# Four of 128 stores on 14 DMA engines, in shares of nine partitions

## The chip, the cores and the metric

One core of one Trainium2 chip. The metric is the device time of one execution, in microseconds (us), median of the timed runs. The kernel of before was run again beside every kernel, on the same chip.

## The reference, cut to what matters

Attention with one query per head, and its gradients. There are 2 x 32 = 64 heads, 8192 keys each, head size 128, all bf16.

```python
def _fwd_reference(q, k, v):
    scale = q.shape[-1] ** -0.5
    scores = jnp.einsum("bhqd,bhkd->bhqk", q, k) * scale
    p = _softmax(scores, axis=-1)
    return jnp.einsum("bhqk,bhkd->bhqd", p, v)
# returned: the output, and the gradients of q, k and v for a given grad_out
```

K and V are 64 x 2 MB each and are read once. dK and dV have the same size and are written once. That is 268 MB in and 268 MB out, with little arithmetic per byte.

## The kernel before

Per head, K and V are loaded whole into SBUF (128 partitions x 16 KB) from the SyncE queue. Twelve such tiles rotate. When scores, softmax and the reductions are done, VectorE overwrites the K tile with dK and the V tile with dV, in place, and GpSimd issues the store. The next load into that tile waits until the store has landed.

```python
CH = 16                      # rows of one partition per chunk; a tile has NT = 64
NTILE = 12                   # K and V tiles in rotation
load_eng = nc.sync
store_eng = nc.gpsimd

def load(i, w, pieces=(NCH,)):           # w: 0 is K, 1 is V
    h = heads[i]
    t = kvp.tile([P, NT, D], BF16, tag=f"kv{slot_of(i, w)}", name="kvt")
    ...
        pin(load_eng.dma_start(out=t[:, n0:n1, :], in_=src[:, n0:n1, :]))

def outer(i, w, c, ends):
    ...                                  # VectorE writes chunk c of dK or dV into the tile
    if c + 1 in ends:
        at = ends.index(c + 1)
        b0, b1 = (ends[at - 1] if at else 0) * CH, (c + 1) * CH
        dst = (dv_v if w else dk_v)[i]
        pin(store_eng.dma_start(out=dst[:, b0:b1, :], in_=h.tile[w][:, b0:b1, :]))

whole = [NCH]                            # one 2 MB store per tile
last = list(range(1, NCH + 1))           # the last head's are cut in four
...                                      # (all else is cut: transposes, scores, softmax, dQ)
```

## Time and profile before

| | before |
|---|---|
| time, first three runs | 1306.17 us median (1304.99 to 1306.63) |
| span of the profiled run | 1303.1 us |
| busiest compute engine | PE, 89% |
| DMA | 414 GB/s over the span |

The page of the kernel before has busy time by engine in part 1. Part 2 cuts the span into 40 equal slices: the DMA digits are the busy share of the 16 DMA engines in tenths (9 is 90% or more), and the row below is what they moved.

```profile
span 1303.1 us, 42566 instructions
PE 1154.0 (89%) x19268; PEld 873.0 (67%) x19268; DVE 937.5 (72%) x2122; ACT 974.8 (75%) x641; POOL 72.4 (6%) x142
DMA  9999999999999999999999999999999999999965
GB/s 390 423 427 427 427 427 427 428 426 430 427 427 427 427 427 429 427 428 427 429 427 427 429 427 424 418 420 425 421 416 420 419 421 421 418 421 422 394 281 206
```

The DMA engines bound the kernel. The last three slices tell more: 394, 281 and 206 GB/s means that some engines have nothing left to do while another still works.

The waits of the SyncE queue in before (who waits, for whom, us in all, times, longest) show that loads wait for stores:

```profile
SPq L89 <- DMA out_dram<-kvt: 1140.6, 116, 24.2
```

The chain of work that ended last, near its end, in before (start, us, what): the last head's compute hangs on the landing of the last load of V.

```profile
1215.54 49.35 DMA kvt<-in_v_dram
1264.94 1.49 PE tp L166 x16
```

The page has no view by DMA engine, but the trace keeps the sixteen completion steps of each copy, one per engine. Read from there, for 2 MB stores counted from 0 (us from the start of the span):

```
store   first step   15th step   16th step   16th - 15th
  8        125.9       128.9       130.4        1.5
 24        281.5       287.5       293.0        5.6
 64        672.2       684.8       698.5       13.7
112       1155.0      1161.6      1185.1       23.4
```

One engine, the laggard, falls behind by 0.21 us per store (23.4 - 1.5 over 104 stores), while the other fifteen lie within some 15 us. Every load waits for that engine. It gets through a head in 20.25 us; over its 32 packets of 16 KB per head that makes 633 ns each, where the median packet takes 611. At the end of the last load of V, when only it still has load packets, its last 13 took 618 to 655 ns.

### The profile page before, as it was taken

Reading aid. Unit: us, or ns where it says so; the run is one execution under the profiler, and the core shown is the slowest. Engines: PE = TensorE matmul, PEld = TensorE weight load, DVE = VectorE, ACT = ScalarE, POOL = GpSimd, SP = SyncE. Lnnn points to the kernel's source line nnn. Section 1 sums busy time; section 2 is a strip of 40 time slices with the busy share of each in tenths; the row PEclk is TensorE's granted clock in tenths of the full one; section 3 lists DMA queues with packets and bytes.
Section 4 is the critical chain, followed back from the end, with each engine's and each line's share of the span. In section 5 each row is a group of like instructions: output and inputs, shape, how many; then the busy total and the mean of one; then the engine's idle time right before and its main releaser. Section 6 shows DMA issues by size and latency. Waiting matters only on the chain.

```text
span 1303.1 us, 42566 instructions
## 1 busy us (share of the span) xinstructions
PE 1154.0 (89%) x19268; PEld 873.0 (67%) x19268; DVE 937.5 (72%) x2122; ACT 974.8 (75%) x641; POOL 72.4 (6%) x142
## 2 busy tenths in 40 slices
PE   6999998889898888988989888989898898888984
PEld 5777776667676666666766666667676676666662
DVE  2888887677776777767777677676776767777776
ACT  6888887777787777777778777777777777777771
POOL 0000000000000000000000000000000000000001
PEclk9999999899898999989989999898898989999986
DMA  9999999999999999999999999999999999999965
GB/s 390 423 427 427 427 427 427 428 426 430 427 427 427 427 427 429 427 428 427 429 427 427 429 427 424 418 420 425 421 416 420 419 421 421 418 421 422 394 281 206
DMA packets 38517, 539.67 MB, mean 414 GB/s; under 512 B 4544, under 2 KB 4544, under 8 KB 5824
## 3 DMA queue, kind: packets, MB, share of 16 engines
q1 hardware_dynamic: 19040, 268.51, 48.9%
q0 software_dynamic: 19296, 268.44, 48.7%
q8 instruction: 150, 2.46, 0.7%
q14 instruction: 31, 0.25, 0.0%
HBM read 268.47 MB, written 268.47 MB: 412 GB/s over the span
## 4 chain that ended last, share of the span: by engine, by line
issue 80%; DMA 11%; POOL 4%; DVE 2%; PE 1%; POOLq 0%; SPq 0%; DVEq 0%
DMA kvt<-in_v_dram 8%; POOL out_dram L390 4%; DMA out_dram<-kvt 3%; DVE kvt L376 1%; PE tp L166 1%; POOLq L390 0%; PE acc L321 0%; DVE sel L344 0%; PE dpw L177 0%; SPq L89 0%; SPq L96 0%; DVE sel L338 0%; PE sw L177 0%; PE acc L358 0%; DVE pair L252 0%
## 5 line engine op out<-in xcount | busy, mean ns | idle before, releaser
L168 ACT COPY ev<-tp 128x2048 bf16<-128x2048 bf16 x512 | 954.0, 1865 | 300.3 <-PE tp L166 290.6
L166 PE MATMUL tp<-ident_bf,kvt 128*128 128x128 bf16 x8192 | 573.4, 226 | 108.9 <-DMA kvt<-in_v_dram 91.1
L376 DVE TENSOR_TENSOR kvt<-qb,pair 128x2048 bf16<-128x2048 bf16 x512 | 621.1, 1214 | 0.2
L166 PEld LDWEIGHTS <-kvt 128*128 128x128 bf16 x8192 | 501.4, 102 | 116.2 <-DMA kvt<-in_v_dram 95.8
L177 PEld LDWEIGHTS <-ev 128*128 128x128 bf16 x8192 | 242.8, 96 | 211.2 <-issue 164.4
L321 PE MATMUL acc<-kvt,dS_pad 128*64 128x512 bf16 x1024 | 177.2, 430 | 1.3 <-DVE dqT L361 1.3
L321 PE MATMUL acc<-kvt,E_pad 128*64 128x512 bf16 x1024 | 159.8, 392 | 0.0
L177 PE MATMUL dpw<-qdT,ev 128*128 128x1 bf16 x4096 | 140.9, 164 | 12.0 <-DVE qb L159 10.7
L189 DVE TENSOR_REDUCE mp<-sw 128x1 f32<-128x64 f32 x64 | 14.3, 224 | 186.5 <-PE sw L177 186.5
L344 DVE SCALAR_TENSOR_TENSOR sel<-acc,diag,sel 128x128 f32<-128x128 f32 x384 | 134.6, 351 | 13.6
L177 PE MATMUL sw<-qdT,ev 128*128 128x1 bf16 x4096 | 142.5, 164 | 1.1 <-ACT ev L168 1.1
L390 POOL DMA_DIRECT2D out_dram<-kvt x134 | 71.3, 532 | 1219.2 <-DVE kvt L376 1186.8
L321 PEld LDWEIGHTS <-dS_pad 128*64 128x64 bf16 x1024 | 38.5, 113 | 26.9 <-issue 9.4
L229 DVE CAST E_pad<-E_f 128x64 bf16<-128x64 f32 x64 | 12.5, 195 | 60.6 <-ACT E_f L220 60.6
L321 PEld LDWEIGHTS <-E_pad 128*64 128x64 bf16 x1024 | 36.3, 108 | 21.0 <-issue 0.2
L358 PE MATMUL acc<-ones,sel 128*128 128x1 f32 x256 | 43.3, 239 | 6.2 <-DVE sel L344 6.2
L264 PE MATMUL dpw<-ld,ones 128*128 128x1 f32 x256 | 46.3, 250 | 0.1
L338 DVE TENSOR_SCALAR sel<-acc,diag 128x128 f32<-128x128 f32 x128 | 44.0, 344 | 0.0
L358 PEld LDWEIGHTS acc<-ones,sel 128*128 128x128 f32 x256 | 39.0, 193 | 7.3 <-DVE sel L344 7.3
L235 DVE CUSTOM_DVE_ANT_0 junk<-E_f,dpw 128x64 bf16<-128x64 f32 x64 | 14.1, 220 | 40.2 <-PE dpw L177 40.2
L159 DVE CAST qb<-dpw 128x128 bf16<-128x128 f32 x128 | 35.4, 277 | 6.0 <-PE dpw L150 6.0
L264 PEld LDWEIGHTS dpw<-ld,ones 128*128 128x128 f32 x256 | 38.2, 188 | 0.5 <-DVE ld L235 0.5
(42 smaller groups left out, 303.2 us busy)
## 6 DMA issues: line engine op xcount, KB each, us to landing
out_dram<-kvt POOLq DMA_DIRECT2D x126, 2048.0 KB, 40.4
kvt<-in_v_dram SPq DMA_DIRECT2D x64, 2048.0 KB, 49.3
kvt<-in_k_dram SPq DMA_DIRECT2D x63, 2048.0 KB, 49.4
out_dram<-kvt POOLq DMA_DIRECT2D x8, 512.0 KB, 11.3
kvt<-in_k_dram SPq DMA_DIRECT2D x2, 512.0 KB, 4.5
kvt<-in_k_dram SPq DMA_DIRECT2D x1, 1024.0 KB, 7.1
out_dram<-nat SPq DMA_DIRECT2D x2, 16.0 KB, 5.0
qd_nat<-in_q_dram SPq DMA_DIRECT2D x1, 16.0 KB, 6.8
```

The costliest lines, as they stand in the source:

```text
L159: pin(nc.vector.tensor_copy(out=h.qb[w][:], in_=h.qbp))
L166: pin(nc.tensor.transpose(tp[:, t, :], src[:, c * CH + t, :], ident_bf[:]))
L168: pin(nc.scalar.copy(out=ev[:], in_=tp[:]))
L177: nc.tensor.matmul(dst[:, c * CH + t : c * CH + t + 1], lhsT=ev[:, t, :], rhs=qdT[:, w, i : i + 1], start=True, stop=True,)
L189: pin(nc.vector.reduce_max(out=h.mp[:], in_=h.s, axis=AX.X))
L264: nc.tensor.matmul(out, lhsT=ones[:].to_broadcast([P, P]), rhs=col, start=True, stop=True)
L321: nc.tensor.matmul(h.acc[w][g : g + CW, :], lhsT=wts[:, n0 : n0 + CW], rhs=rows[:, n0 : n0 + QT, :].rearrange("p n d -> p (n d)"), start=( ...
L338: nc.vector.tensor_scalar(out=h.sel[:], in0=block, scalar1=diag[:, 0:1], scalar2=None, op0=ALU.mult)
L344: nc.vector.scalar_tensor_tensor(out=h.sel[:], in0=block, scalar=diag[:, b : b + 1], in1=h.sel[:], op0=ALU.mult, op1=ALU.add,)
L358: nc.tensor.matmul(h.acc[w][:, 0:1], lhsT=h.sel[:], rhs=ones[:], start=True, stop=True)
L376: nc.vector.tensor_tensor(out=h.tile[w][:, n0 : n0 + CH, :].rearrange("p n (e t) -> p n e t", t=2), in0=h.qb[w][:] .rearrange("p (e t) -> ...
L390: pin(store_eng.dma_start(out=dst[:, b0:b1, :], in_=h.tile[w][:, b0:b1, :]))
```

## The change

Its intent is to take work off that slow engine. For four heads' dK stores (heads 9, 23, 37, 51), four pieces of two partitions move GpSimd's round-robin cursor over the DMA engines from 0 to 8. Then the other 126 partitions go out as one copy. 126 = 14 x 9, so by the rule that the prediction cites it runs on 14 engines from the cursor on: 8 to 15 and 0 to 5. Engines 6 and 7 are left with one 4 KB piece each in place of 128 KB. `max_dma_last_dim`, in bytes, is given half a row, so rows are cut in two.

```diff
-            pin(store_eng.dma_start(out=dst[:, b0:b1, :], in_=h.tile[w][:, b0:b1, :]))
+            if w == 0 and i % 14 == 9 and ends is whole:
+                spread(dst, h.tile[w])
+            else:
+                pin(store_eng.dma_start(out=dst[:, b0:b1, :], in_=h.tile[w][:, b0:b1, :]))
+
+    def spread(dst, t):
+
+        def put(parts, r0, r1):
+            pin(
+                store_eng.dma_start(
+                    out=dst[parts, r0:r1, :],
+                    in_=t[parts, r0:r1, :],
+                    max_dma_last_dim=(r1 - r0) * D,
+                )
+            )
+
+        pin(store_eng.inc_swdge_sem([], [], mode="reset_dge_cursor"))
+        for m in range(4):
+            put(slice(P - 2, P), m * NT // 4, (m + 1) * NT // 4)
+        put(slice(0, P - 2), 0, NT)
```

## The prediction

> **What bounds it now.** The DMA engines, and among them one. The page's DMA row stands at 9 tenths in 38 of 40 slices, at 414 GB/s over the span; the busiest compute engine, PE, is at 89%. In the SP queue's waits, loads wait 1140.6 of 1303 us for stores to land, so each load starts when the slowest share of an earlier store is in.
>
> The trace keeps sixteen completion steps of every DMA. In store 8 the sixteenth comes 1.5 us after the fifteenth; in store 24, 5.6; in store 64, 13.7; in store 112, 23.4. So one engine falls behind 0.22 us per store all through; the other fifteen lie within some 10 us. Heads come 20.25 us apart by the laggard. A 16 KB packet takes 611 ns at the median; the laggard's 32 packets a head give 20.25/32 = 633 ns. The last load of V has its fifteenth step at 1243.0 us and its sixteenth at 1264.9; in the chain of waits the final head's compute (38 us) hangs on that landing. The last store: fifteenth step 1295.1, sixteenth 1301.1. In the last three slices bandwidth falls to 394, 281 and 206 GB/s: fifteen engines run dry.
>
> **What the change does.** For four heads' dK (9, 23, 37, 51) engines 6 and 7 carry 4 KB each in place of 128 KB. The Trainium skill (DMA: Bandwidth & Descriptors, section "Why a DMA increments its semaphore by 16 and not by 1") says that GpSimd copies not spread over all 16 run on k consecutive engines from a cursor, k the largest divisor up to 16. Four two-partition pieces move the cursor from 0 to 8; then 126 partitions on 14 engines take 8 to 15 and 0 to 5. The cap on the last dim halves the rows (an 8 KB packet costs 309 ns here, so no loss) and presumably keeps the copy off the all-sixteen path. No trace here shows the cursor yet.
>
> Which engine lags cannot be read here. The same page ("Latency and other measured facts") calls 7 and 15 usually slower; the change is sensible only if the laggard is 7 or 6.
>
> - Removed from the laggard: 4 x 124 KB = 31 packets x 633 ns = 19.6 us.
> - Added to the others: 16 or 20 KB per store, 4 to 5 packets x 611 ns = 2.4 to 3.1 us in all.
> - Added on GpSimd: four issues of 0.53 us and a cursor reset per such store; it idles 7 to 12 us between stores. Off the path.
>
> **On the critical path.** The laggard would land the last load at about 1245.3, the others at 1243.0 + 3 = 1246: balanced, about 19 us gained. The tail gives 2 to 4 us more, since the final stores no longer queue behind a backlog; the small dQ and O stores then end it (now 1298.7 against 1301.1). Together about 21.5 us.
>
> **Prediction: 1284.5 us**, 80% range 1280 to 1302. Faster by over 2%: 0.07; within 2%: 0.91; slower: 0.02.
>
> **What would show it.** After each of the four stores the gap from fifteenth to sixteenth step drops by about 5 us, ending near 0 to 3; heads come every 19.9 us on average; the last three slices keep higher bandwidth.
>
> **What would make it wrong.** The laggard is another engine, or cursor or split differ (one in five): then the lag stays or grows, and the time is 1303 to 1312. Nine-partition shares might crowd SBUF ports and make packets slower. The second-slowest engines may lag more once pushed.

## More of the kernel before

The DMA view of before lists issues by line: what moves, the issuing queue, how many, KB each, and the median time from issue to landing.

```profile
out_dram<-kvt POOLq DMA_DIRECT2D x126, 2048.0 KB, 40.4
kvt<-in_v_dram SPq DMA_DIRECT2D x64, 2048.0 KB, 49.3
kvt<-in_k_dram SPq DMA_DIRECT2D x63, 2048.0 KB, 49.4
```

A 2 MB copy at full rate needs about 5 us (2.1 MB / 427 GB/s). Here each takes 40 to 49 us, so several copies stand in the queues of every engine at once.

The waits of GpSimd in before show that it waits for VectorE's results only, never for a landing:

```profile
POOL out_dram L390 <- DVE kvt L376: 1186.8, 127, 32.2
```

## The result, and the profile after

| | before | after |
|---|---|---|
| time | 1305.58 us median (1304.88 to 1306.63, 4 runs) | 1315.10 us median (1314.79 to 1315.35, 4 runs) |
| span of the profiled run | 1303.1 us | 1312.9 us |
| ratio | | 1.0072, 95% interval 1.0055 to 1.0090 |

A ratio is the mean time of one kernel's runs over that of the other's runs of the same rounds, so it is not quite the ratio of the medians. Executions over 1.5% slower than the fastest of the same kernel are left out of the means. The change made the kernel 0.7% slower: 9.5 us lost where 21.5 were to be gained.

The page after, the same lines as of before:

```profile
span 1312.9 us, 42614 instructions
PE 1143.8 (87%) x19268; PEld 867.7 (66%) x19268; DVE 936.5 (71%) x2122; ACT 975.4 (74%) x641; POOL 83.0 (6%) x158
DMA  9999999999999999999999989999999989999993
GB/s 389 426 428 427 426 427 427 427 426 428 428 428 428 428 428 410 425 425 427 429 428 428 427 355 386 418 427 427 429 428 428 428 331 387 423 427 427 428 405 120
```

There are dips at slices 16, 24 and 25, and 33 and 34 (410; 355, 386; 331, 387), and the tail is still there (120). The DMA view after:

```profile
out_dram<-kvt POOLq DMA_DIRECT2D x122, 2048.0 KB, 62.1
kvt<-in_v_dram SPq DMA_DIRECT2D x64, 2048.0 KB, 19.0
kvt<-in_k_dram SPq DMA_DIRECT2D x63, 2048.0 KB, 19.3
out_dram<-kvt POOLq DMA_DIRECT2D x4, 2016.0 KB, 48.7
out_dram<-kvt POOLq DMA_DIRECT2D x16, 8.0 KB, 54.5
```

Stores now stand 62 us in the queues and loads only 19. The waits of the SyncE queue and of GpSimd after:

```profile
SPq L89 <- DMA out_dram<-kvt: 1165.6, 124, 24.4
```

```profile
POOL out_dram L393 <- DVE kvt L376: 903.6, 101, 32.6
POOL out_dram L393 <- DMA out_dram<-kvt: 80.5, 11, 11.0
POOL out_dram L393 <- issue: 50.9, 7, 11.3
POOL out_dram L399 <- DMA out_dram<-kvt: 41.2, 5, 9.6
```

By these lines GpSimd now waits 121.7 us (80.5 + 41.2) for stores to land; the page of before has no such wait. Around the second changed head its timeline after shows it (start, us busy, idle before and what ended it):

```profile
477.09 0.55 POOL L399 DMA_DIRECT2D out_dram<-kvt  x1 [3.59 <-DMA out_dram<-kvt]
487.19 0.55 POOL L399 DMA_DIRECT2D out_dram<-kvt  x1 [9.56 <-DMA out_dram<-kvt]
497.04 0.77 POOL L399 DMA_DIRECT2D out_dram<-kvt  x1 [9.30 <-DMA out_dram<-kvt]
507.45 0.58 POOL L393 DMA_DIRECT2D out_dram<-kvt  x1 [9.64 <-DMA out_dram<-kvt]
```

The trace says why: the stores use eight semaphores in turn, and GpSimd may not reuse one before the store that had it has landed. Five copies in a row take five of the eight while four to seven stores are still in flight. Where the profile prints "DVE" or "issue" after such a wait, the instruction before each of these issues is GpSimd's own wait on a store semaphore. So the printed sum is too low. Counted from the trace instead, as the idle time before every issue that comes within 0.7 us of the landing of the store eight issues earlier, it is 33 issues and 204.3 us (before: one, 1.9 us). This count is used below.

Which engine lags? The completion steps (16th minus 15th, us, by store of the head order; the pieces of a cut store counted as one) and, with them, those of the first experiment:

```
store              18    24    46    52    74    80   102   108   120
before            3.5   5.6   9.9  11.5  15.3  17.5  21.1  21.9  22.9
after             3.4   5.4   9.7  19.9  24.5  26.4  34.3  32.0  20.3
e1 (below)        3.5   1.3   4.0   0.1   4.4   3.1   1.2   3.0   2.2
```

The changed stores are numbers 19, 47, 75 and 103. After the second the lag jumps from 9.7 to 19.9 us, after the third it grows by 1.9, after the fourth it is 2.3 less, and after none does it drop by the 5 us that were expected: the laggard was not relieved. The packet records say more. Each small piece carries data on two engines, and on the fourteen others a packet of 8 B stands in its place. At the last changed head, the latest of these packets, 30 us behind all others and so the laggard's, come at:

```
8 B at 1105.8    8 B at 1107.1    4096 B at 1108.3    8 B at 1109.7      (us, after)
```

So the laggard carried data in the third of the four pieces. The third pair from cursor 0 is 4 and 5. At heads 23 and 37 the order is the same (527.3, 528.6, data at 529.8, 531.2; and 818.2, 819.5, data at 820.7, 821.5). The change left out the pair next to it.

### The profile page after: what moved, and what is told of

Read it like the earlier page. It is cut to its first block, busy times and chain, and to the rows that moved or that the text cites. A ratio compares the mean times of both kernels' runs of the same rounds, so it can differ in the third digit from the quotient of the medians.

```text
span 1312.9 us, 42614 instructions
## 1 busy us (share of the span) xinstructions
PE 1143.8 (87%) x19268; PEld 867.7 (66%) x19268; DVE 936.5 (71%) x2122; ACT 975.4 (74%) x641; POOL 83.0 (6%) x158
## 4 chain that ended last, share of the span: by engine, by line
DMA 36%; another core or an unknown queue 35%; issue 17%; PE 7%; DVE 2%; SPq 1%; POOL 1%; POOLq 0%
DMA kvt<-in_v_dram 17%; DMA out_dram<-kvt 14%; DMA kvt<-in_k_dram 5%; PE tp L166 3%; PE acc L321 2%; DVE kvt L376 1%; SPq L89 1%; PE dpw L177 1%; POOL out_dram L393 1%; PE sw L177 1%; DVE sel L344 0%; POOL out_dram L399 0%; DVE sel L338 0%; PE dpw L264 0%
## 5 line engine op out<-in xcount | busy, mean ns | idle before, releaser
L321 PE MATMUL acc<-kvt,dS_pad 128*64 128x512 bf16 x1024 | 172.8, 421 | 1.8 <-DVE dqT L361 1.8
```

The costliest lines, as they stand in the source:

```text
L321: nc.tensor.matmul(h.acc[w][g : g + CW, :], lhsT=wts[:, n0 : n0 + CW], rhs=rows[:, n0 : n0 + QT, :].rearrange("p n d -> p (n d)"), start=( ...
```

## The experiments

Engines are named by the cursor's count: 0 is where it starts after a reset. No run shows that this count is the chip's own numbering.

### e1: the other pair

```diff
-        for m in range(4):
+        for m in range(3):
             put(slice(P - 2, P), m * NT // 4, (m + 1) * NT // 4)
         put(slice(0, P - 2), 0, NT)
+        put(slice(P - 2, P), 3 * NT // 4, NT)
```

> Same five copies per chosen head as the change, same bytes, but the big copy is issued fourth and one small piece last, so the pair left out is 4 and 5. Theory A (wrong pair: in the trace of the change the lagging engine carried data in the third small piece, so it is 4 or 5 by the cursor's count): the gap from fifteenth to sixteenth step drops by about 5 us at each of the four heads instead of growing by 10, and the laggard saves 19 us; with GpSimd's waits still there I expect 1290 to 1300 us. Rival (the pair does not matter, the loss is all GpSimd's blocked issue or the nine-partition shares): 1313 to 1317 us.

Measured: 1289.19 us median (1288.02 to 1290.40), ratio 0.9882 (0.9868 to 0.9897). Theory A holds, and the time is just under its range. The lag stays at 0.1 to 4.4 us (row e1 of the table above). The same five copies, the same bytes, as long waits of GpSimd for landings (34 issues, 209.6 us, against 33 and 204.3), and only another pair of engines: the sign turns. Its GB/s row:

```profile
GB/s 389 423 427 427 426 427 428 427 427 427 427 427 427 428 428 426 421 427 427 427 427 428 427 427 397 411 427 428 428 427 429 428 412 403 422 427 427 427 427 230
```

In the last three slices it moves 427, 427 and 230 GB/s, where before moved 394, 281 and 206: the sixteen engines now finish nearly together. The wrong pair is shown.

### e2, e3: two copies in place of five

The first changed head sets the cursor, with five copies (e2) or four (e3). Later heads need two: the small copy of 2 partitions runs on the pair, the big one takes the next 14 engines, and 2 + 14 = 16 brings the cursor back.

```diff
-        pin(store_eng.inc_swdge_sem([], [], mode="reset_dge_cursor"))
-        for m in range(4):
-            put(slice(P - 2, P), m * NT // 4, (m + 1) * NT // 4)
+        if first:                        # i == 9
+            pin(store_eng.inc_swdge_sem([], [], mode="reset_dge_cursor"))
+            for m in range(3):           # e3: range(2)
+                put(slice(P - 2, P), 16 * m, 16 * m + 16)
+            put(slice(P - 2, P), 48, NT) # e3: 32
+        else:
+            put(slice(P - 2, P), 0, NT)
         put(slice(0, P - 2), 0, NT)
```

> Pair 6 and 7 as in the change, but with two copies per head (one small, one big) after the first such head, where five set the cursor. Theory B (five copies in a row take five of the eight store semaphores, so GpSimd stands until old stores have landed, stores and then loads start late and all engines run dry): the dips to 331 to 410 GB/s vanish, GpSimd's waits on landed stores shrink from 120 us to under 50, and the time is 1307 to 1310 us, the remainder being 4 extra shares of 16 KB on the lagging engine (2.5 us). Rival (the shares of nine partitions or the 8 KB packets cost the time): stays at 1313 to 1317 us.

> Both: pair 4 and 5 left out and two copies per head (four at the first). If A and B hold, the laggard saves 28 packets x 633 ns = 18 us, no dips, and the tail gives 2 to 4 us: 1284 to 1289 us. If only A holds: about as e1. If only B holds: 1306 to 1309 us.

Measured: e2 1313.62 us (1311.52 to 1317.26), ratio 1.0072 (1.0055 to 1.0090); e3 1290.58 us (1288.28 to 1292.67), ratio 0.9887 (0.9871 to 0.9904). e2 lands in the range of its rival, not of theory B. The deepest dips are gone (lowest slice before the tail 396 GB/s), and its page prints few waits on landings:

```profile
POOL out_dram L393 <- DMA out_dram<-kvt: 24.2, 4, 11.0
POOL out_dram L399 <- DMA out_dram<-kvt: 5.2, 2, 2.7
```

But by the count above 19 issues still waited 137.7 us, so e2 took away only a third of the waits and is a weak test. e3 waited 75.4 us where e1 waited 209.6, and is as fast as e1, not faster. Fewer waits gained nothing here; e4, next, tests the waits directly.

### e4, e5, e11: the side costs alone

No engine is left out, all shares are even and at their usual partitions. e4 cuts the store of the four heads in five copies, e5 cuts its rows in half, e11 does both.

```diff
+        # e4 (e11: the same, with max_dma_last_dim=(r1 - r0) * D)
+        for r0, r1 in ((0, 2), (2, 4), (4, 6), (6, 8), (8, NT)):
+            pin(store_eng.dma_start(out=dst[:, r0:r1, :], in_=t[:, r0:r1, :]))
+        # e5
+        pin(store_eng.dma_start(out=dst, in_=t[:], max_dma_last_dim=NT * D))
```

> For the same four heads the store is cut into five plain 128-partition copies (four of 2 rows, one of 56), all 16 engines, no cursor, no padding. Theory B alone: the dips and GpSimd's waits are there without any uneven share: 1309 to 1315 us. Rival (the loss of the change comes from the uneven shares): 1305 to 1307 us.

> For the change's four heads the store stays one even copy over 128 partitions and 16 engines, but with rows cut into 8 KB packets. Theory (an engine takes turns packet by packet, so half-size store packets give loads twice the bytes for a while; this only shifts stores back and loads forward, no work is added): 1304 to 1307 us, loads landing sooner after issue and stores later. Rival (half-size packets by themselves slow the lagging engine, and explain part of the 9 us): 1308 to 1312 us.

> Five even copies over 128 partitions for the change's four heads, all with rows cut in half: the two side costs of the change together, no engine left out. If they add (e4 2.2 us, e5 1.8 us): 1308 to 1310 us, which with 3.2 us for 80 KB more on the lagging engine accounts for 7 to 8 of the 9.4 us that the change lost. If they do not add: 1306 to 1307 us.

Measured: e4 1306.86 us, ratio 1.0018 (1.0003 to 1.0033); e5 1306.35 us, 1.0014 (0.9999 to 1.0029); e11 1307.31 us, 1.0017 (1.0000 to 1.0033). So the two costs come to about 2 us, alone or together. e4 has GpSimd's waits (32 issues, 211.9 us, as many as after) and the dips in full:

```profile
POOL out_dram L398 <- DMA out_dram<-kvt: 68.9, 9, 9.9
POOL out_dram L393 <- DMA out_dram<-kvt: 27.2, 5, 9.6
GB/s 389 422 427 429 426 426 428 426 429 427 428 428 428 428 427 427 427 428 427 428 428 426 428 383 401 423 427 427 427 427 428 428 333 397 426 427 427 427 422 122
```

383 and 333 GB/s, much as after, yet the kernel loses 2 us. So GpSimd's waits are not what the change lost. Counting the sixteenth steps of loads and stores together, by bytes, the laggard of e4 stays within about 2 us of before all through. So the dips are mostly the other fifteen engines, using up early the slack that they otherwise idle away at the end.

e5 in the DMA view:

```profile
out_dram<-kvt POOLq DMA_DIRECT2D x126, 2048.0 KB, 57.4
kvt<-in_v_dram SPq DMA_DIRECT2D x64, 2048.0 KB, 31.6
```

Stores 40.4 to 57.4 us, loads 49.3 to 31.6, from four stores with half-size packets. The Trainium skill (DMA: Bandwidth & Descriptors, section "Queues, rings and completion order") says that a DMA engine takes turns between its queues packet by packet. This agrees: while store packets are half as big, loads get the larger part of the bytes. What one queue gains the other loses, and the total hardly moves.

### e6, e7: one engine alone

Six heads; 120 partitions run on 15 engines, eight each; engine 4 (e6) or 5 (e7) is left out of that copy. The 8 other partitions move the cursor.

```diff
-        for m in range(4):
-            put(slice(P - 2, P), m * NT // 4, (m + 1) * NT // 4)
-        put(slice(0, P - 2), 0, NT)
+        put(slice(P - 5, P), 0, NT)          # e7: P - 6
+        put(slice(0, P - 8), 0, NT)
+        put(slice(P - 8, P - 5), 0, NT)      # e7: P - 6
```

> Six heads; 15 engines carry 8 partitions each of 120, engine 4 alone (by the cursor's count) is left out of the big copy and carries 32 KB in all. If 4 is the laggard: 6 x 96 KB = 36 packets x 633 ns = 22.8 us less on it, nobody else left idle: 1281 to 1287 us, below e1. If the laggard is 5, it carries 16 KB more each time: 3.8 us by bytes, 1308 to 1320 us.

> The same with engine 5 left out alone. If 5 is the laggard: 1281 to 1287 us; if it is 4: 1308 to 1320 us. Exactly one of this and the run before should gain.

Measured: e6 1293.13 us (1289.46 to 1299.06), ratio 0.9917 (0.9886 to 0.9947); e7 1314.48 us (1313.69 to 1318.37), ratio 1.0086 (1.0068 to 1.0104). Exactly one gains: the slow engine is 4, by the cursor's count. e6 missed the expected 1281 to 1287.

### e8: the change at early heads

```diff
-            if w == 0 and i % 14 == 9 and ends is whole:
+            if w == 0 and i in (6, 9, 12, 15):
```

> The change as it is, pair 6 and 7, five copies, but at heads 6, 9, 12 and 15, before the other engines have run far ahead. If the cost on the laggard is the bytes alone (20 KB per head, 3.2 us in all): 1307 to 1310 us. If each such store costs the same 2.4 us wherever it stands: 1312 to 1316 us. In the trace of the change the laggard lost 0.8 and 1.1 us at the first two heads and 3.3 and 5.5 us at the last two, so I expect the former.

Measured: 1315.87 us (1315.25 to 1317.05), ratio 1.0088 (1.0073 to 1.0103). A miss, the branch that was thought less likely: the loss is as large as at the change's own heads. Counted as for e4, the laggard stands 10.8 us behind the kernel of before by 540 us, with the last changed head past, and still 10.0 us behind at 1060 us. So it is the changed stores that cost, about 2.5 us each, not the run between them; and 20 KB more on the laggard (0.8 us at 633 ns per 16 KB) is a third of that.

### e9, e10: other heads for the right pair

e9 is e3 at heads 0, 10, 20, 30, 40; e10 is e1 at heads 3, 6, 9, 12.

```diff
-            if w == 0 and i % 14 == 9 and ends is whole:
+            if w == 0 and i in (0, 10, 20, 30, 40):    # e9
+            if w == 0 and i in (3, 6, 9, 12):          # e10
```

> Candidate for the best version: pair 4 and 5 left out at five heads (0, 10, 20, 30, 40), four copies at head 0 where no store semaphore is in use yet, two copies after. The laggard sheds 568 KB, 34.7 packets x 633 ns = 22 us, less about 1 us per store for packets and copies: 1284 to 1290 us. If idle time of the healthy partner engine 5 costs as much as it saves, it stays at 1289 to 1293 us, as e1 and e3.

> e1 with its four heads moved early and close (3, 6, 9, 12). Same bytes off engine 4. If only the bytes on the slowest engine count: 1288 to 1293 us like e1. If engine 4 must be relieved when it is already behind (else the relief is lost in idle time while it waits for the others): 1293 to 1303 us.

Measured: e9 1289.28 us (1286.76 to 1295.70), ratio 0.9883 (0.9853 to 0.9913); e10 1292.10 us (1291.40 to 1293.89), ratio 0.9899 (0.9884 to 0.9914). Where the relief stands matters little. No run of these comes below 1286.

### e12, e13: even shares at shifted partitions

What was open by then: with 3.2 us for bytes and about 2 us for side costs, some 4 us of the 9.5 had no owner. The packet records gave a hint. Store packets (8 or 16 KB, between 150 and 1230 us, none within 1.3 us after an instruction fetch, which is queue q8) that took over 15% longer than the usual 309 or 611 ns, and their excess summed over all engines:

```
                                      packets   excess, us   time against before
even, usual partitions   before          45        11.3
                         e4              35         9.6        +0.2%
                         e5              47        15.5        +0.1%
                         e11             43        10.2        +0.2%
shares of nine           after          111        33.0        +0.7%
                         e2             148        60.4        +0.7%
                         e8             177        71.6        +0.9%
```

In e2, 22 of them took exactly 1208 ns, in e8 ten: almost exactly twice 611, as if two engines shared something. After itself has hardly any of that length. The Trainium skill (SBUF — State Buffer, section "Door 1: The DMA port swizzle") gives SBUF sixteen DMA ports of eight partitions, and the page DMA: Bandwidth & Descriptors (section "The descriptor swizzle") has each engine of a usual 128-partition copy at a port of its own. On that map nine partitions in a row do not fit: an engine walks over other engines' ports. To test it without uneven bytes, e12 stores the four heads as 112 partitions (7 per engine) and 16 (1 per engine), in full rows on all 16 engines; e13 does so for 63 heads.

```diff
+        for parts in (slice(0, P - 16), slice(P - 16, P)):
+            pin(store_eng.dma_start(out=dst[parts], in_=t[parts]))
```

> For the change's four heads the store is two copies of full 16 KB rows: 112 partitions (7 per engine) and 16 partitions (1 per engine). Every engine carries its usual 128 KB and none is left out, no cursor, no half rows; only which partitions an engine reads is shifted against the usual share. Theory (shares that do not fit the usual partition groups make engines meet at the same SBUF port once they are out of step, and stretch store packets): stretched store packets rise from 10 to 15 us of engine time (before, e4, e5, e11) to over 30 us, and the time is 1307 to 1312 us. Rival (only unequal bytes matter): 10 to 15 us and 1304 to 1307 us.

> The same at the dK store of 63 heads, to multiply the effect by 16. Theory of crowded ports: stretched store packets over 300 us of engine time and at least 1320 us. Rival (only bytes matter): 1304 to 1310 us, two copies in place of one.

Measured: e12 1315.26 us (1313.69 to 1316.72), ratio 1.0070 (1.0055 to 1.0085), with 199 stretched packets and 97.8 us of excess; its time is above even the theory's range. e13 1406.94 us (median of three fast runs, 1400.35 to 1414.95; the slow one took 1432.0), ratio 1.0747 (1.0716 to 1.0779), with 2132 packets and 1302.8 us. The rows after the first of e13's page show it over the whole run:

```profile
DMA  9999999999999999999999999999999999999993
GB/s 391 420 424 419 411 400 405 403 399 389 388 383 385 389 388 384 387 379 383 368 372 384 395 393 378 373 378 372 375 382 388 394 383 394 386 397 385 403 311 136
```

The DMA engines are "90% or more" busy in all slices but the last and from the tenth slice on move mostly 370 to 400 GB/s in place of 427: busy, with longer packets. e12 costs as much as the whole change, with even bytes, no cursor and full rows. Its page has one wait of GpSimd for a landing, 4.4 us in the last head, and loads and stores stand in the queues about as long as before:

```profile
out_dram<-kvt POOLq DMA_DIRECT2D x122, 2048.0 KB, 43.4
kvt<-in_v_dram SPq DMA_DIRECT2D x64, 2048.0 KB, 46.7
out_dram<-kvt POOLq DMA_DIRECT2D x4, 1792.0 KB, 43.4
POOL out_dram L393 <- DMA out_dram<-kvt: 4.4, 1, 4.4
```

Counted as for e4, the laggard of e12 falls back around each of the four stores: from 0.5 to 1.6 us behind before, from 0.8 to 4.0, from 5.0 to 7.0 and from 7.4 to 9.2.

### e14, e15: the same, by port

```diff
+        for parts in (slice(32, 96), slice(0, 32), slice(96, P)):   # e14
+        for parts in (slice(0, 64), slice(64, P)):                  # e15
+            pin(store_eng.dma_start(out=dst[parts], in_=t[parts]))
```

> Three even copies: partitions 32 to 95 (4 per engine; by the skill's table sixteen different ports), 0 to 31 and 96 to 127 (2 per engine, two engines to a port). Half the bytes free of sharing. Port theory: stretched store packets clearly fewer than in e15, under 120 us of engine time, 1308 to 1314 us. Rival (any unusual share costs the same per byte): same stretch and time as e15.

> Two even copies: partitions 0 to 63 and 64 to 127 (4 per engine; by the table each copy reaches only eight ports, two engines to each, all the time). Port theory: the most stretch of the four-head runs, over 150 us of engine time, with packets near twice 611 ns, and 1313 to 1325 us. Rival: like e14 and e12, about 98 us and 1315 us.

Measured: e14 1306.23 us (1305.99 to 1307.07), ratio 1.0015 (0.9999 to 1.0031), 43 stretched packets, 14.8 us of excess, as with the usual shares. e15 1312.82 us (1309.11 to 1313.22), ratio 1.0055 (1.0031 to 1.0079), 175 packets, 87.9 us. Both are even, and e14 has the more copies. In e14's middle copy, if shares are handed out in order, every engine reads at the port that the page gives it in a usual copy; in e15 half the engines read at another's. The order is as the port theory has it, the sizes are not: e14 came out below its range, and e15 stretched no more than e12, as its rival said. By the table e14's two outer copies put two engines to a port as well, and they did not stretch. Nor does any run part the SBUF side from the DRAM side: the same edits change which rows of dK each engine writes, and a limit there is a rival that no run tests. What e12 to e15 show is that shifted shares cost time; that the ports are the reason is argued.

### e16: a relief that should fit the ports

Ten heads; 60 partitions on the 15 engines other than 4, four each; small copies for the rest.

```diff
+        put(slice(31, 36), 0, NT)
+        put(slice(36, 96), 0, NT)
+        for parts in (slice(0, 31), slice(96, P)):
+            pin(store_eng.dma_start(out=dst[parts], in_=t[parts]))
```

> Ten heads; per head a small copy of 5 partitions moves the cursor to 5, then 60 partitions (36 to 95) run on 15 engines without engine 4, then 31 and 32 partitions on all. Engine 4 sheds 3 of its 8 partitions, 48 KB a head, 480 KB in all: 30 packets x 633 ns = 19 us. If the ports are the missing part: stretched store packets under 25 us of engine time, 1283 to 1289 us. If the extra copies cost as much as the ports did: 1289 to 1296 us.

Measured: 1297.75 us (1295.80 to 1303.01), ratio 0.9959 (0.9929 to 0.9990), 166 stretched packets, 65.8 us. A miss. But the copy that was made to fit did not stretch: here only the 60- and 5-partition copies have 8 KB packets, and 2 of these 1160 took over 15% longer, against 49 of 1008 in after and 87 of 1020 in e3. The stretch is in 16 KB packets, those of the other two copies and of the ordinary stores. Why they stretch here and hardly do in e14, with much the same outer copies, is open. GpSimd also waits longer for landings here than in any other run with few changed heads (77 issues, 562.0 us).

## Why the prediction was wrong

- "One engine falls behind", and everything waits for it: right. The lag is there in before and after, and relieving that engine made the kernel 1.2% faster (e1).
- "The change is sensible only if the laggard is 7 or 6": this is the step that failed. It was inferred from the change's intent and from a general remark in the Trainium skill, and given four chances in five; no line of the trace stood behind it. The laggard is engine 4 by the cursor's count (the third small piece in the trace after; e1 against after; e6 against e7). So "removed from the laggard: 19.6 us" was 0, and the laggard got 80 KB more.
- "The cursor ... four two-partition pieces move the cursor from 0 to 8": right as far as it was tested. The laggard carried data in the third small piece, and e1, e6 and e7 steered by the count.
- "The laggard is another engine ... the time is 1303 to 1312": the right branch, mis-sized. It held the bytes, 2.4 to 3.1 us (3.2 at the laggard's own pace). Measured: 9.5.
- "Nine-partition shares might crowd SBUF ports": named, with no number. Shifted partitions alone cost 8.9 us (e12, difference of medians) at the same four heads, more than any other term. How much of the change's 9.5 us this is, and whether the ports are the reason, is not shown: the change has 22 us more of stretched packets than before, e12 has 87 more.
- "An 8 KB packet costs 309 ns here, so no loss", and GpSimd's issues "off the path": small misses. Half rows cost 1.8 us (e5) and five copies 2.2 us (e4); together 1.3 us (e11, difference of medians of 1307.31 and 1306.00). The intervals of e5 and e11 reach to no loss at all.
- The terms do not add: bytes 3.2, side costs about 2 and shifted partitions 8.9 would be 14 us, and 9.5 were lost. How they overlap stays open, and so does whether crowding takes the same share of the laggard's time in the change as in e12: the change has 33.0 us of stretched packets, e12 97.8.
- With the right pair, the prediction's sum would have been 21.5 us of gain, and e1 gained 15.4 (1304.61 - 1289.19). Stretched packets (124, 46.9 us) and side costs are in e1 too and may be the missing 6 us, but no run shows a relief free of them.

## What to carry to other kernels

When one DMA engine sets the pace, find out which one before moving work off it. The completion steps show that there is a laggard; a small copy on a known pair, and whether the late packet carries data, shows its number. And watch which partitions each engine is given: even shares at shifted partitions cost 8.9 us at four stores here (e12), more than half of the 15.4 us that the right relief gained in all (e1). Judge a dip in DMA bandwidth by what the slowest engine does in it, not by its depth. And where a profile names no wait, look at the semaphore that the issue itself waits for.

## What the Trainium skill lacked or had wrong

- DMA: Bandwidth & Descriptors, "Latency and other measured facts": engines 7 and 15 are called usually slower. Here the slow one is engine 4 by the cursor's count (e6 against e7, on one chip), and one of the pair 4 and 5 on two others (e1, e9): 633 ns against 611 per 16 KB packet, 23.4 us behind by store 112. Leaving out 6 and 7 gained nothing (after, e2, e8). That the cursor counts as the page does is not shown.
- The same page, "Why a DMA increments its semaphore by 16 and not by 1": the cursor rule held. It does not say that engines left out still get a tiny packet for each share's packet (224 of 8 B for 16 small pieces, 14 each; 144 of 4 B for four big ones, 18 on each of two engines), which take turns with real packets: the laggard's four in after came 1.2 to 1.4 us apart.
- The same page, "The descriptor swizzle": it gives the map for 128 partitions and leaves open what copies of other shapes cost among others in flight. 112 + 16 partitions in place of 128 cost 0.7% at four stores of 128 and 7.5% at 63 (e12, e13); 64 + 32 + 32 cost 0.15% (e14).
- SBUF — State Buffer, "Door 1": it gives the ports that one copy reaches and its rate alone. Nothing there tells how much packets stretch beside other copies: e15's two halves had 87.9 us of stretched packets, e14's half and two quarters 14.8.
- No page has the limit that this program's stores met: eight semaphores in turn, so a burst of five copies makes GpSimd wait up to 11.0 us at a time for old stores to land.
